# Linformer attention and a gated feed-forward layer in one kernel: single load buffers, q of batch 1 transposed by DMA, denominators once per head, projections moved, 64x32 tiles

## The chip, the core and the metric

The kernel runs on one core of one Trainium2 chip. The metric is the device time of one execution in microseconds. Before the change the median of eight runs is 517.92 us (517.8 to 520.12).

## What is computed

Eight batches of eight heads, 1024 positions, head size 64. k and v are projected along the sequence to 64 rows, q attends to these 64 rows, and the result, with the heads side by side (8192 tokens of 512 numbers), goes through a feed-forward layer of 2048 with a quick-gelu.

```python
k_proj = np.einsum('ks,bhsd->bhkd', E, k)
v_proj = np.einsum('ks,bhsd->bhkd', F, v)
scores = scale * np.matmul(q, k_proj.transpose(0, 1, 3, 2))
scores = scores - np.max(scores, axis=-1, keepdims=True)
attn = np.exp(scores)
attn = attn / (np.sum(attn, axis=-1, keepdims=True) + 1e-09)
attn_out = np.matmul(attn, v_proj)
...
x = attn_out.transpose(0, 2, 1, 3).reshape(B * S, H * D)
h = x @ w_in
out = (h * (1.0 / (1.0 + np.exp(-1.702 * h)))) @ w_out
```

The kernel leaves out the maximum and the small addend in the denominator; inputs and outputs are float32, the matmuls work on bfloat16.

## The kernel before

The 8192 tokens are worked in 16 blocks of 512, two to a batch. Block j runs the feed-forward layer for its tokens: `ffn1` (L295), sixteen groups of four full matmuls whose results ACT turns into gelu, then `ffn2` (L313), eight half groups of eight full matmuls, two for each of four output tiles. The matmuls of a block are 128, each 128x128 by 512 columns. The attention of later blocks is placed between these groups by hand: `at(j, slot, f)` (L344) files a function under block j and a slot, and the main loop (L419) calls what is filed after each group. Slots 0 to 15 follow the groups of ffn1, `O` = 16 is the slot after the first half group of ffn2, `O + 7` the last. Every engine works through its own instructions in this program order; nothing reorders them.

For one block h of 512 tokens the attention is:

- `proj(b)` (L139), once per batch: k and v times E and F, 16 matmuls of 128x64 tiles in pairs. `kv_out(b)` (L184) casts the results on DVE, and for b above 1 SP issues a DMA transpose of k into `kts`. For batch 1, `k_tr` (L161) does it on PE.
- q: for batches 0 and 1 `q_tr` (L195) transposes on PE through PSUM with a DVE copy (L211), in four steps per batch; from batch 2 on `q_dma` (L214) is one DMA transpose on the SP queue.
- `scores(h, u)` (L227), u = 0, 1: `four` (L221), that is four matmuls on 64x64 tiles, then two exponentials on ACT into `expT` (L239).
- `norm(h, u)` (L250), for h from 3: `four` with a matrix of ones for the denominators, which come out repeated over 64 rows each (`d_ps`), `four` with v for the values (`n_ps`), and on DVE a reciprocal of 512 columns (L259) and a product (L260) for each of two tiles, into `xT`.
- For h up to 2, `tok` (L267) and `x_tr` (L282) do the same with tokens on the rows.

A burst is what one slot holds of scores and norm. From block 3 on there are two bursts in each block, in slots O and O + 5, each with scores of block j + 3 and norm of block j + 2.

Loads are issued by POOL in program order (`load`, L65): k and v of a batch by one DMA each, q by eight. `ldpool` has two buffers for each of k, v and q (and one, `q0_sb`, for q of batch 0), and the loads of batch b are called two batches ahead; a load waits until its buffer was read for the last time. The SP queue carries the outputs of each block (L340) and the DMA transposes, in order.

PSUM is eight banks: four for `f_ps` (feed-forward, scores, projections and transposes in turn), two for `d_ps`, two for `n_ps`. A tile that is asked for takes the buffer that was given back first in program order.

Of the kernel before, what the change touches and what calls it, by code (L numbers as in the profile page):

```python
# [9 lines left out]
F32 = mybir.dt.float32  # L10
# [7 lines left out]
def kernel(ctx, tc, q, k, v, E, F,  # L18
# [18 lines left out]
    ldpool = ctx.enter_context(tc.tile_pool(name="ldpool", bufs=2))  # L37
# [4 lines left out]
    ps_n = ctx.enter_context(tc.tile_pool(name="ps_n", bufs=2, space=PSUM))  # L42
    ctx.enter_context(tc.manual_schedule())
# [8 lines left out]
    def load_kv(src, dst, b, name, hs=H, js=0, jn=J):  # L52
        if b not in dst:
            dst[b] = ldpool.tile([P, H, J, D], BF16, name=name, bufs=1 if name == "q0_sb" else 2)
        sv = src[b].rearrange("h (p j) d -> p h j d", p=P)
        for h, n in [(h, hs) for h in range(0, H, hs)] if isinstance(hs, int) else hs:
            nc.gpsimd.dma_start(out=dst[b][:, h:h + n, js:js + jn], in_=sv[:, h:h + n, js:js + jn])  # L57
# [79 lines left out]
    kvps, kbs, qT, expT, xT = {}, {}, {}, {}, {}  # L137
# [57 lines left out]
    def q_tr(b, g):  # L195
        def go():
            if g == 0:
                qT[b] = att.tile([P, J, HP, P], BF16, name="qT")
            t_ps = f_tile([P, 2, HP, P], BF16)
            for jj in range(2):  # L200
                j = 2 * g + jj
                if b == 0:
                    for h in range(H):
                        r = h % 2 * D
                        nc.tensor.transpose(t_ps[r:r + D, jj, h // 2, :], qt[0][:, h, j, :], ident)  # L205
                else:
                    for p in range(HP):
                        nc.tensor.transpose(
                            t_ps[:, jj, p, :],
                            qt[b][:, j, 2 * p:2 * p + 2, :].rearrange("s t d -> s (t d)"), ident)  # L210
            nc.vector.tensor_copy(qT[b][:, 2 * g:2 * g + 2], t_ps)  # L211
        return go

    def q_dma(b):  # L214
        def go():
            qT[b] = att.tile([P, J, HP, P], BF16, name="qT")
            nc.sync.dma_start_transpose(out=qT[b].rearrange("r j p s -> r (j p) s"),
                                        in_=qt[b].rearrange("s j h d -> s (j h d)"))
        return go

    def four(outs, lhsTs, rhss):  # L221

        for i, ro in ((0, (LO, HI)), (1, (HI, LO))):
            for ri, r in zip((LO, HI), ro):
                nc.tensor.matmul(outs[i][r], lhsTs[i][ri], rhss[i][ri], start=True, stop=True)  # L225

    def scores(h, u, half=None):  # L227
        b, c = divmod(h, NB2)
        j0, n = (c * JB, JB) if half is None else (c * JB + half * JB // 2, JB // 2)
        ts = slice(j0 * P - c * TB, (j0 + n) * P - c * TB)  # L230

        def go():
            if h not in expT:
                expT[h] = att.tile([P, HP, TB], BF16, name="expT", bufs=3)
            s_ps = [f_tile([P, n * P]) for _ in range(2)]
            four(s_ps, [kts[b % 2][:, 2 * u + i, :] for i in range(2)],
                 [qT[b][:, j0:j0 + n, 2 * u + i, :] for i in range(2)])
            for i in range(2):
                nc.scalar.activation(expT[h][:, 2 * u + i, ts], s_ps[i], AF.Exp, scale=scale)  # L239
        return go  # L240
# [8 lines left out]

    def norm(h, u):  # L250
        def go():
            e = [expT[h][:, 2 * u + i, :] for i in range(2)]
            d_ps = [ps_d.tile([P, TB], F32, name="d_ps") for _ in range(2)]
            four(d_ps, [ones, ones], e)
            n_ps = [ps_n.tile([P, TB], F32, name="n_ps") for _ in range(2)]
            four(n_ps, [vqs[h // NB2 % 2][:, 2 * u + i, :] for i in range(2)], e)
            for i in range(2):
                rden = att.tile([P, TB], F32, name="rden")
                nc.vector.reciprocal(rden, d_ps[i])  # L259
                nc.vector.tensor_tensor(x_of(h)[:, 2 * u + i, :], n_ps[i], rden, op=ALU.mult)  # L260
# [83 lines left out]
    def at(j, slot, *fs):  # L344
        fill.setdefault((j, slot), []).extend(fs)
# [9 lines left out]
    for u in range(2):  # L355
        scores(0, u, 0)()
    v_out(0, proj0(1, 4, 2), 2, 1)
    for p in range(3):
        tok(0, p, 0)()
    v_out(0, proj0(1, 6, 2), 3, 1, nc.scalar.copy)  # L360
    for p in range(3):
        x_tr(0, p, 0)()
    tok(0, 3, 0)()
    q_tr(0, 1)()
# [17 lines left out]
    at(1, 4, proj(1))  # L382
    at(1, 5, kv_out(1))
    at(1, 7, lambda: k_tr(1, kbs[1], 0), q_dma(2))
    for g in range(4):
        at(1, 8 + 2 * g, q_tr(1, g))
# [8 lines left out]
    at(2, 1, norm(3, 0))  # L395
    at(2, 11, norm(3, 1))
    for b in range(2, B):
        j = max(2, NB2 * b - 3)
        at(j, 2, proj(b))
        at(j, 3, kv_out(b))  # L400
        if b > 2:
            at(NB2 * b - 4, O, q_dma(b))
    for j in (1, 2):
        at(j, O + 5, gelu_table)
    at(2, O + 5, norm(4, 0))
    at(3, 4, norm(4, 1))
    for j in range(3, NBLK - 2):
        for u in range(2):
            if j + 3 < NBLK:
                at(j, O + 5 * u, scores(j + 3, u))  # L410
            at(j, O + 5 * u, norm(j + 2, u))
        if j + 3 < NBLK:
            at(j, O + 6, gelu_table)
# [48 lines left out]
```

The softmax here doesn't subtract the row's maximum and nothing guards it: scores larger than these inputs give would overflow.

## Time and profile before

| what | value |
|---|---|
| median of 8 runs | 517.92 us |
| the profiled execution | 517.8 us |
| its span, first to last instruction | 516.0 us |
| granted TensorE clock, mean | 0.999 |
| first ffn1 matmul (block 0) | 21.03 us |
| blocks 1, 2, 3 begin | 55.4, 90.84, 123.96 us |
| matmuls of ffn1 and ffn2, L301 and L333, busy | 226.6 and 225.1 us |
| DVE reciprocals L259 | 52 of 3353 ns |
| DMA moved | 53.78 MB, 104 GB/s over the span |

The span is what the profile shows from the first instruction to the last; the 1.8 us around it belong to the measured time. A start time in the text is counted from the start of the span. In the profile an engine's busy time is the union of its instructions; PE's matmuls overlap, so what a group of them costs is read from the distance between starts and not from the length of one. "PEld" are the weight loads, which run beside matmuls. Where an instruction waited, the profile names in brackets for how long and for whom. For DMAs, SPq and POOLq rows show when the queue's engine issued them, and "us to landing" how long from there to the completion.

### The profile page before, as it was taken

What the parts mean: (1) busy time and instruction counts of PE and PEld (TensorE: products, weight loads), DVE (VectorE), ACT (ScalarE), POOL (GpSimd) and SP (SyncE); (2) the same over time, 40 slices, a digit from 0 to 9 for tenths busy, and PEclk for the clock granted to TensorE, in tenths of its full rate; (3) what the DMA queues carried; (4) which work ended last, traced back from release to release, by engine and by line L of the source; (5) the groups of instructions that cost most, each with busy time, mean ns of one, the idle gap of its engine ahead of it and who ended that gap; (6) DMA issues with size and microseconds to landing.
All of it is one profiled execution on the core that took longest, in us unless ns stands there. A gap on an engine that the chain in (4) does not pass through costs nothing.

```text
span 516.0 us, 6679 instructions
## 1 busy us (share of the span) xinstructions
PE 504.6 (98%) x2806; PEld 233.4 (45%) x2856; DVE 251.2 (49%) x231; ACT 263.8 (51%) x439; POOL 77.3 (15%) x96
## 2 busy tenths in 40 slices
PE   7899999999999999999999999999999999999997
PEld 3584454434444444444444444444444444444444
DVE  2633324766684672818557282755818275560000
ACT  1575454555646456474555645465473646344351
POOL 7442620831510024000510000000000000000000
PEclk9999999999999999999999999999999999999999
DMA  9999999999996039550694211060200101010102
GB/s 169 197 203 206 219 176 154 196 188 159 239 152 163 1 93 171 108 123 0 152 176 120 50 49 39 0 164 0 85 2 1 81 1 81 1 82 1 81 1 82
DMA packets 113950, 53.78 MB, mean 104 GB/s; under 512 B 87680, under 2 KB 111488, under 8 KB 112000
## 3 DMA queue, kind: packets, MB, share of 16 engines
q0 software_dynamic: 84384, 29.37, 50.4%
q1 hardware_dynamic: 29456, 23.73, 16.7%
q8 instruction: 22, 0.36, 0.3%
q10 hardware_dynamic: 80, 0.26, 0.2%
q14 instruction: 8, 0.07, 0.0%
HBM read 59.24 MB, written 16.78 MB: 147 GB/s over the span
## 4 chain that ended last, share of the span: by engine, by line
PE 85%; DMA 11%; POOL 2%; issue 1%; DVE 0%; DVEq 0%; POOLq 0%
PE f_ps L333 40%; PE f_ps L301 38%; DMA v_sb<-in_v_dram 7%; DMA q_sb<-in_q_dram 5%; PE f_ps L144 2%; PE f_ps L225 2%; PE d_ps L225 1%; PE n_ps L225 1%; POOL q_sb L63 1%; PE f_ps L325 1%; POOL k_sb L57 0%; POOL v_sb L57 0%; PE n_ps L287 0%; PE d_ps L272 0%; POOL q_sb L57 0%
## 5 line engine op out<-in xcount | busy, mean ns | idle before, releaser
L259 DVE RECIPROCAL rden<-d_ps 128x512 f32<-128x512 f32 x52 | 174.4, 3353 | 149.0 <-PE d_ps L225 149.0
L301 PE MATMUL f_ps<-xT,w_in_sb 128*128 128x512 bf16 (+1 forms) x1066 | 226.6, 366 | 1.2
L333 PE MATMUL f_ps<-w_out_sb,gT 128*128 128x512 bf16 x981 | 225.1, 379 | 1.7 <-issue 0.3
L304 ACT ACTIVATE gT<-f_ps 128x512 bf16<-128x512 f32 (+1 forms) x268 | 153.6, 575 | 85.2 <-PE f_ps L301 84.3
L301 PEld LDWEIGHTS <-w_in_sb 128*128 128x128 bf16 x1088 | 104.6, 98 | 115.9 <-issue 4.3
L333 PEld LDWEIGHTS <-gT 128*128 128x128 bf16 x1008 | 95.8, 98 | 120.3 <-issue 11.0
L336 ACT COPY o_sb<-f_ps 128x512 f32<-128x512 f32 x63 | 36.9, 586 | 133.5 <-PE f_ps L333 120.1
L63 POOL DMA_DIRECT2D q_sb<-in_q_dram x56 | 49.1, 907 | 67.4 <-DMA k_sb<-in_k_dram 27.4
L239 ACT ACTIVATE expT<-f_ps 128x512 bf16<-128x512 f32 (+1 forms) x68 | 35.2, 575 | 14.1 <-PE f_ps L225 14.1
L260 DVE TENSOR_TENSOR xT<-n_ps,rden 128x512 bf16<-128x512 f32 x52 | 36.0, 692 | 5.4
L327 DVE COPY o_sb<-f_ps 128x256 f32<-128x256 f32 x1 | 0.4, 425 | 50.9 <-PE f_ps L325 50.9
L57 POOL DMA_DIRECT2D k_sb<-in_k_dram x9 | 7.9, 874 | 102.9 <-PE f_ps L144 101.2
L239 ACT ACT_TABLE_LOAD x13 | 16.7, 1283 | 4.7 <-PE f_ps L225 4.5
L243 ACT ACT_TABLE_LOAD x14 | 18.0, 1283 | 0.2
L225 PE MATMUL f_ps<-qT,kt 64*64 64x512 bf16 (+1 forms) x136 | 13.8, 386 | 0.4 <-ACT expT L239 0.4
L144 PE MATMUL f_ps<-v_sb,eft 128*64 128x512 bf16 x56 | 13.4, 382 | 0.0
L144 PE MATMUL f_ps<-k_sb,eft 128*64 128x512 bf16 x56 | 13.4, 382 | 0.0
L211 DVE COPY qT<-f_ps 128x1024 bf16<-128x1024 bf16 x8 | 5.5, 692 | 12.4 <-PE f_ps L205 6.8
L277 DVE RECIPROCAL rd<-d_ps 128x4 f32<-128x4 f32 x22 | 3.8, 175 | 15.5 <-PE d_ps L272 15.4
L225 PEld LDWEIGHTS <-kt 64*64 64x64 bf16 x136 | 4.0, 103 | 14.3 <-issue 13.8
L225 PE MATMUL d_ps<-expT,ones 64*64 64x512 bf16 x104 | 10.2, 381 | 0.0
L225 PE MATMUL n_ps<-expT,vq 64*64 64x512 bf16 x104 | 10.0, 376 | 0.0
(57 smaller groups left out, 128.1 us busy)
## 6 DMA issues: line engine op xcount, KB each, us to landing
out_dram<-o_sb SPq DMA_DIRECT2D x15, 1024.0 KB, 4.2
k_sb<-in_k_dram POOLq DMA_DIRECT2D x7, 1024.0 KB, 13.8
v_sb<-in_v_dram POOLq DMA_DIRECT2D x7, 1024.0 KB, 10.8
q_sb<-in_q_dram POOLq DMA_DIRECT2D x56, 128.0 KB, 11.1
w_in_sb<-in_moe_w_in_dram POOLq DMA_DIRECT2D x8, 256.0 KB, 12.4
w_out_sb<-in_moe_w_out_dram POOLq DMA_DIRECT2D x4, 512.0 KB, 15.0
k_sb<-in_k_dram POOLq DMA_DIRECT2D x2, 512.0 KB, 7.5
out_dram<-o_sb SPq DMA_DIRECT2D x3, 256.0 KB, 2.0
```

The costliest lines, as they stand in the source:

```text
L57: nc.gpsimd.dma_start(out=dst[b][:, h:h + n, js:js + jn], in_=sv[:, h:h + n, js:js + jn])
L63: nc.gpsimd.dma_start(out=qt[b][:, j], in_=qv[:, j])
L144: nc.tensor.matmul(kvps[b][r], eft[:, j, e * KP:(e + 1) * KP], (kt, vt)[e][b][:, :, j, :], start=(j == 0), stop=(j == J - 1))
L225: nc.tensor.matmul(outs[i][r], lhsTs[i][ri], rhss[i][ri], start=True, stop=True)
L239: nc.scalar.activation(expT[h][:, 2 * u + i, ts], s_ps[i], AF.Exp, scale=scale)
L243: nc.scalar.preload_act_table(AF.Gelu_apprx_sigmoid)
L259: nc.vector.reciprocal(rden, d_ps[i])
L260: nc.vector.tensor_tensor(x_of(h)[:, 2 * u + i, :], n_ps[i], rden, op=ALU.mult)
L301: nc.tensor.matmul(h_ps, w_in_sb[:, kc, fc * P:(fc + 1) * P], xT[j][:, kc, ts], start=(kc == 0), stop=(kc == KC - 1))
L304: nc.scalar.activation(gts[j][:, fc, ts], h_ps, AF.Gelu_apprx_sigmoid)
L333: nc.tensor.matmul(o_ps[n], gts[j][:, fc, n * P:(n + 1) * P], w_out_sb[:, fc, :], start=(fc == 0), stop=(fc == FC - 1))
L336: nc.scalar.copy(osb[j][:, n, :], o_ps.pop(n))
```

## The change

It has six parts.

- k, v and q have one load buffer each. A batch's loads therefore wait until the batch before was projected (k, v) and transposed (q).
- q of batch 1 is transposed by two DMAs on SP, each for half of the tokens, filed in slot (1, 1); the branch of `q_tr` for later batches goes, and `q_dma(2)` moves from (1, 7) to (1, O + 7).
- `four` becomes `eight`: the same products with tiles of 64 rows and 32 columns, two for each 64x64 tile.
- From h = 4 on `norm` is split. `sums(h)` gets the denominators of all eight heads with one set of eight 64x32 tiles, takes two reciprocals on DVE, writes four rows of them to DRAM (`rdr`) and reads them back repeated over 64 rows (`rbc`), both by DMAs on SP. `values(h, u)` multiplies with v and then, on DVE, with `rbc`. sums(h) is filed in (h - 2, O), values(h, 0) in (h - 2, O + 6), values(h, 1) in (h - 1, O).
- `proj(1)` moves to (1, 10), `proj(3)` to (3, 6) beside values(4, 0), and proj(4) to proj(7) from (2b - 3, 2) to (2b - 4, O + 6), ahead of that slot's burst. The second burst moves from O + 5 to O + 6. `q_dma(b)` of batches 4 to 7 moves from (2b - 4, O) to (2b - 4, 2).
- At the start, tok and x_tr of block 0's first half are ordered differently among the projections of v.

```diff
-    ldpool = ctx.enter_context(tc.tile_pool(name="ldpool", bufs=2))
+    ldpool = ctx.enter_context(tc.tile_pool(name="ldpool", bufs=1))
+    dram = ctx.enter_context(tc.tile_pool(name="dram", bufs=2, space=bass.MemoryType.DRAM))
...
-            dst[b] = ldpool.tile([P, H, J, D], BF16, name=name, bufs=1 if name == "q0_sb" else 2)
+            dst[b] = ldpool.tile([P, H, J, D], BF16, name=name)
...
-                j = 2 * g + jj
-                if b == 0:
-                    for h in range(H):
-                        r = h % 2 * D
-                        nc.tensor.transpose(t_ps[r:r + D, jj, h // 2, :], qt[0][:, h, j, :], ident)
-                else:
-                    for p in range(HP):
-                        nc.tensor.transpose(
-                            t_ps[:, jj, p, :],
-                            qt[b][:, j, 2 * p:2 * p + 2, :].rearrange("s t d -> s (t d)"), ident)
+                for h in range(H):
+                    r = h % 2 * D
+                    nc.tensor.transpose(t_ps[r:r + D, jj, h // 2, :], qt[0][:, h, 2 * g + jj, :], ident)
             nc.vector.tensor_copy(qT[b][:, 2 * g:2 * g + 2], t_ps)
         return go
 
-    def q_dma(b):
-        def go():
-            qT[b] = att.tile([P, J, HP, P], BF16, name="qT")
-            nc.sync.dma_start_transpose(out=qT[b].rearrange("r j p s -> r (j p) s"),
-                                        in_=qt[b].rearrange("s j h d -> s (j h d)"))
-        return go
-
-    def four(outs, lhsTs, rhss):
+    def q_dma(b, j0=0, n=J):
+        def go():
+            if j0 == 0:
+                qT[b] = att.tile([P, J, HP, P], BF16, name="qT")
+            nc.sync.dma_start_transpose(out=qT[b][:, j0:j0 + n].rearrange("r j p s -> r (j p) s"),
+                                        in_=qt[b][:, j0:j0 + n].rearrange("s j h d -> s (j h d)"))
+        return go
+
+    def eight(outs, lhsTs, rhss):
         for i, ro in ((0, (LO, HI)), (1, (HI, LO))):
-            for ri, r in zip((LO, HI), ro):
-                nc.tensor.matmul(outs[i][r], lhsTs[i][ri], rhss[i][ri], start=True, stop=True)
+            for c in range(0, KP, 32):
+                for ri, r in zip((LO, HI), ro):
+                    nc.tensor.matmul(outs[i][r.start + c:r.start + c + 32], lhsTs[i][ri, c:c + 32], rhss[i][ri],
+                                     start=True, stop=True)
 
...
+    def sums(h):
+
+
+        def go():
+            d_ps = [ps_d.tile([P, TB], F32, name="d_ps") for _ in range(2)]
+            for p in range(HP):
+                for e in range(2):
+                    r = HI if (p + e) % 2 else LO
+                    nc.tensor.matmul(d_ps[e][32 * p:32 * p + 32], ones[r, :32], expT[h][r, p, :], start=True, stop=True)
+            rden = att.tile([P, 2, TB], F32, name="rden")
+            for e in range(2):
+                nc.vector.reciprocal(rden[:, e, :], d_ps[e])
+            rdr = dram.tile([HP, 2, TB], F32, name="rdr")
+            nc.sync.dma_start(out=rdr, in_=rden[0:P:32])
+            rbc[h] = att.tile([P, HP, TB], F32, name="rbc")
+            for e, r in enumerate((LO, HI)):
+                nc.sync.dma_start(out=rbc[h][r], in_=rdr[None, :, e, :].to_broadcast([D, HP, TB]))
+        return go
+
     def norm(h, u):
         def go():
             e = [expT[h][:, 2 * u + i, :] for i in range(2)]
             d_ps = [ps_d.tile([P, TB], F32, name="d_ps") for _ in range(2)]
-            four(d_ps, [ones, ones], e)
+            eight(d_ps, [ones, ones], e)
             n_ps = [ps_n.tile([P, TB], F32, name="n_ps") for _ in range(2)]
-            four(n_ps, [vqs[h // NB2 % 2][:, 2 * u + i, :] for i in range(2)], e)
+            eight(n_ps, [vqs[h // NB2 % 2][:, 2 * u + i, :] for i in range(2)], e)
             for i in range(2):
-                rden = att.tile([P, TB], F32, name="rden")
-                nc.vector.reciprocal(rden, d_ps[i])
-                nc.vector.tensor_tensor(x_of(h)[:, 2 * u + i, :], n_ps[i], rden, op=ALU.mult)
+                rd = att.tile([P, TB], F32, name="rdn")
+                nc.vector.reciprocal(rd, d_ps[i])
+                nc.vector.tensor_tensor(x_of(h)[:, 2 * u + i, :], n_ps[i], rd, op=ALU.mult)
+        return go
+
+    def values(h, u):
+        def go():
+            n_ps = [ps_n.tile([P, TB], F32, name="n_ps") for _ in range(2)]
+            eight(n_ps, [vqs[h // NB2 % 2][:, 2 * u + i, :] for i in range(2)],
+                  [expT[h][:, 2 * u + i, :] for i in range(2)])
+            for i in range(2):
+                nc.vector.tensor_tensor(x_of(h)[:, 2 * u + i, :], n_ps[i], rbc[h][:, 2 * u + i, :], op=ALU.mult)
         return go
...
     for u in range(2):
         scores(0, u, 0)()
+    for p in range(2):
+        tok(0, p, 0)()
     v_out(0, proj0(1, 4, 2), 2, 1)
-    for p in range(3):
-        tok(0, p, 0)()
+    x_tr(0, 0, 0)()
     v_out(0, proj0(1, 6, 2), 3, 1, nc.scalar.copy)
-    for p in range(3):
-        x_tr(0, p, 0)()
+    tok(0, 2, 0)()
+    x_tr(0, 1, 0)()
     tok(0, 3, 0)()
+    x_tr(0, 2, 0)()
     q_tr(0, 1)()
     x_tr(0, 3, 0)()
...
-    at(1, 4, proj(1))
-    at(1, 5, kv_out(1))
-    at(1, 7, lambda: k_tr(1, kbs[1], 0), q_dma(2))
-    for g in range(4):
-        at(1, 8 + 2 * g, q_tr(1, g))
+    at(1, 10, proj(1))
+    at(1, 11, kv_out(1))
+    at(1, 13, lambda: k_tr(1, kbs[1], 0))
+    at(1, 1, q_dma(1, 0, JB), q_dma(1, JB, JB))
...
-    at(2, 1, norm(3, 0))
-    at(2, 11, norm(3, 1))
-    for b in range(2, B):
-        j = max(2, NB2 * b - 3)
-        at(j, 2, proj(b))
-        at(j, 3, kv_out(b))
-        if b > 2:
-            at(NB2 * b - 4, O, q_dma(b))
     for j in (1, 2):
         at(j, O + 5, gelu_table)
-    at(2, O + 5, norm(4, 0))
-    at(3, 4, norm(4, 1))
-    for j in range(3, NBLK - 2):
+    at(1, O + 7, q_dma(2))
+    at(2, 1, norm(3, 0))
+    at(2, 2, proj(2), kv_out(2))
+    at(2, 11, norm(3, 1))
+    at(2, O + 5, sums(4))
+    at(2, O, q_dma(3))
+    at(3, 6, proj(3), kv_out(3), values(4, 0))
+    for b in range(4, B):
+        j = NB2 * b - 4
+        at(j, O + 6, proj(b), kv_out(b))
+        at(j, 2, q_dma(b))
+    for j in range(3, NBLK - 1):
         for u in range(2):
             if j + 3 < NBLK:
-                at(j, O + 5 * u, scores(j + 3, u))
-            at(j, O + 5 * u, norm(j + 2, u))
+                at(j, O + 6 * u, scores(j + 3, u))
+        at(j, O, values(j + 1, 1))
+        if j + 2 < NBLK:
+            at(j, O, sums(j + 2))
+            at(j, O + 6, values(j + 2, 0))
         if j + 3 < NBLK:
-            at(j, O + 6, gelu_table)
+            at(j, O + 7, gelu_table)
```

## The prediction, made before the changed kernel had run

> **What bounds the kernel now.** I read the page from its first part down: busy time by engine, then the chain that ended last.
>
> ```profile
> span 516.0 us, 6679 instructions
> ...
> PE 504.6 (98%) x2806; PEld 233.4 (45%) x2856; DVE 251.2 (49%) x231; ACT 263.8 (51%) x439; POOL 77.3 (15%) x96
> ...
> PE 85%; DMA 11%; POOL 2%; issue 1%; DVE 0%; DVEq 0%; POOLq 0%
> ```
>
> PE is busy for 98% of the span, carries the chain from 72 us to the end, and DVE and ACT stand at half. So a microsecond taken from PE is a microsecond of the span, unless PE then waits; one taken from DVE is worth nothing by itself. The DMA share of the chain lies before 72 us, where PE is busy too: the chain view follows loads there, but the stage windows below leave PE idle for only 0.2 to 0.4 us per block after the first 21 us.
>
> Next, busy time in windows cut at the starts of the blocks: a block with two bursts of attention work, one that also holds a projection, and one with the feed-forward layer alone. The columns are window, length, then busy time of PE, PEld, DVE, ACT, POOL, clock, DMA share, GB/s.
>
> ```profile
> 155.96:185.34 29.38, 29.22 (x151) 12.85 (x152) 16.01 (x9) 16.43 (x26) 0.00 (x0) 1.00 0.29 72
> 185.34:216.68 31.34, 31.18 (x167) 13.60 (x168) 17.55 (x12) 16.54 (x26) 8.75 (x10) 1.00 1.06 137
> 457.20:484.80 27.60, 27.50 (x127) 12.51 (x128) 4.34 (x3) 11.89 (x20) 0.00 (x0) 1.00 0.10 39
> ```
>
> The last gives the price of a full-size matmul: 27.60/128 = 0.2156 us. The first costs 1.78 us more, for two bursts of three groups each (scores, sums, values). How long one group takes is seen in PE's timeline of one burst:
>
> ```profile
> 262.31 1.24 PE L333 MATMUL f_ps<-w_out_sb,gT 128*128 128x512 bf16 x5
> 263.49 0.41 PE L225 MATMUL f_ps<-qT,kt 64*64 64x512 bf16 x4
> 263.73 0.39 PE L225 MATMUL d_ps<-expT,ones 64*64 64x512 bf16 x4
> 263.94 0.39 PE L225 MATMUL n_ps<-expT,vq 64*64 64x512 bf16 x4
> 264.26 0.60 PE L333 MATMUL f_ps<-w_out_sb,gT 128*128 128x512 bf16 x2
> ```
>
> Groups of four 64x64 tiles start 0.21 to 0.24 us apart: the four run at once, for the price of one matmul. Six groups are 6 x 0.2156 = 1.29 us, so each burst pays (1.78 - 1.29)/2 = 0.24 us to enter and leave the 64x64 layout. A projection adds 31.34 - 29.38 = 1.96 us: 8 pairs x 0.2156 = 1.73, and again 0.23 us for its own layout.
>
> **What the Trainium skill says.** TensorEngine Tiling (Array Packing), Tiling Modes: 64x32 gives eight independent tiles, and changing the tiling mode drains TensorE. The trace agrees on the drain (0.24 us) and on independence for four tiles; it holds no 32-column tile. TensorE: Matmul & The Clock Gate, Measured speedup vs the span model: a packed set lasts one matmul plus about 4 ns per further tile, up to sixteen tiles. The four tiles above agree; for eight I work out an estimate of 16 ns more per group. DMA: Bandwidth & Descriptors, Queues, rings and completion order: each engine takes turns between queues packet by packet. The packet counts of two DMA windows agree, 117 to 121 us with both queues at work (first two lines), and 161 to 164 us with a transpose alone (last line):
>
> ```profile
> q1 hardware_dynamic: 1661, 0.43, 81.1%
> q0 software_dynamic: 1661, 0.21, 79.6%
> ```
> ```profile
> q1 hardware_dynamic: 2593, 0.66, 114.7%
> ```
>
> So a q transpose (1 MB in 256 B packets, 4096) moves 860 packets per us alone, 415 beside a q load, and 146 beside a k or v load (585 in the window 80 to 84 us).
>
> **The change, part by part.**
>
> 1. *q of batch 1.* Four q_tr(1) leave PE:
>
> ```profile
> 65.45 0.61 PE L208 MATMUL f_ps<-ident,q_sb 128*128 128x128 bf16 x8
> 65.89 1.89 PE L301 MATMUL f_ps<-xT,w_in_sb 128*128 128x512 bf16 x8
> ```
>
> From start to start 0.44 us, so 4 x 0.44 = **-1.76 us**. In their place SP issues two half transposes at slot (1,1). They queue behind block 0's output (issued at 56.2) and q1's load (k2's load follows it into the ring at about 58). With 2048 packets each at 860 per us, and 3 us from issue to first packet (157.3 to 160.2 in the DMA records, with the output ahead), the halves land near 67 and 71 us; scores(2,0) needs the first at about 73 us, scores(3,0) the second near 78. Covered by 6 to 7 us. Even a whole transpose at its slow, contended 15 us would end just in time.
>
> 2. *One buffer.* k2 now waits for proj(1), moved to slot 10: that ends near 66.4 us. q2 waits for both transposes (71), then eight loads at 0.88 us issue and 0.85 us of data (128 KB at 155 GB/s), then v2 (1 MB at 205 GB/s, 5 us): lands near 88 us. proj(2) comes at about 92. 4 us to spare. The same chain later: k3 after proj(2) (94), q3 after q_dma(2), v3 about 118, proj(3) at (3,6) near 128. From batch 4 on the loads have over 30 us for 20 us of work. Freed early, the DMA engines are quiet while q1 is transposed.
>
> 3. *Sums once per head.* Per head from 4 to 15 two d groups (64 columns of ones) become one group of eight 64x32 tiles: 12 groups x 0.2156 = **-2.59 us**. DVE loses 24 reciprocals at 3.35 us, 80 us, worth nothing on this path. The new way back is long: from the start T of ffn2, sums end at T+2.6, two products (0.69 each), two reciprocals (3.35 each), rdr (16 KB; 2.0 us, as the 256 KB outputs), and two rbc of 512 KB (5 us; between 4.2, as a 1 MB output, and 8.4): T+17.7. values(h,0) are on PE at T+13.5, so DVE stands some 4 us at its product. Behind it DVE has nothing before the next block's burst at T+31; proj and kv_out are issued ahead of it in the same slot. n_ps is wanted again at T+31. So it costs nothing; if the DMAs took 14 us longer, PE would begin to feel it. On SP, rdr and rbc wait ahead of the block's output, which is ready at T+14.6: two output buffers cover that.
>
> 4. *Merged bursts.* proj(3) to proj(7) move next to a 64x32 burst: three layout changes for four, each half of 0.24: 5 x 0.12 = **-0.6 us**. norm(4,1) at (3,4) is one burst less, values(15,1) at (14,O) one more: zero. With proj in slot O+6, ffn1 of the next block takes the buffer freed first, kvps: DVE has done with it 1.7 us after proj, PE asks after 2.3 us (scores, values, half an ffn2). No stall. The gelu table load after the last ffn2 copy delays the first gelu to about 2.7 us into the block, and PE asks for that buffer at 3.46 us.
>
> 5. *Eight for four.* 70 full and 4 half groups remain (34 of scores, 4 of norm(3), 12 sums, 24 values; 86 before). The cost per group is not in the trace: below, 0, since one, two (proj) and four tiles all start 0.216 us apart; above, 0.2156, if only four run at once. The skill's 4 ns gives 16 ns. I take 5 ns, as that issue time should mostly hide under the group before: **+0.4 us**.
>
> 6. *Start.* tok of pairs 0 and 1 go ahead of proj0(4,2), so DVE's first reciprocal comes about 0.8 us sooner, but its casts of vx for pair 2 and ACT's for pair 3 follow later in the line; x_tr(0,3) moves from 20.9 to about 20.6, and ffn1's last quarter, which waits for ACT's copy at 21.23, with it: **-0.3 us** (from +0.2 to -0.7).
>
> 7. *SP's order in block 2.* Before, the transpose of q2 ran at 75; now it goes out after block 1's output (89.4), ahead of kt(2).
>
> ```profile
> 101.78 1.19 SPq L190 DMA_TRANSPOSE kt<-k_b  x1
> ...
> 109.59 0.11 PEld L225 LDWEIGHTS <-kt 64*64 64x64 bf16 x4 [0.42 <-DMA kt<-k_b]
> ```
>
> kt(2) was just in time before: k_b waits for DVE's norm(3,0), 8.1 us, unchanged. In the new time scores(4,0) come at 107.6. q_dma(2): output packets to 93, 2.6 us alone (2240 packets), 6.7 us beside k3's load (980), 1.0 us alone: ends about 103, SP free at 102.3; kt(2) then takes 2.7 us to its first packet (as at 190.6) and about 1.5 more: 106.5. Expected wait 0; if contention lasts, up to 3.5 us. I take **+0.2**.
>
> **Sum.** -1.76 - 2.59 - 0.6 - 0.3 + 0.4 + 0.2 = -4.65 us. The profiled run took 517.8 us (span 516.0, 1.8 around it): 513.2. The median of the eight runs is 517.92, so this is 4.7 us, 0.9%, below it. I count 0.2%, about 1 us, as what can be told from no change.
>
> **Rivals.**
>
> *A new wait gives part back (14%).* The wait of part 7 at scores(4,0) at its 3.5 us, or a late v2: 513.2 + 3.3 = 516.5. For it: kt(2) was already last before. Against: k_b's own delay is the same, and loads are quieter.
>
> *Eight tiles don't run at once (17%, the slower side).* If the array takes only four at a time, 70 x 0.2156 + 4 x 0.108 = 15.5 us: 513.2 - 0.4 + 15.5 = 528.3. It decides from (4.65 + 0.4)/74 = 68 ns per group on. For it: no 32-column tile in the trace, and every right-hand side is streamed twice. Against: four streams run free of charge, and 16 weight loads and matmuls of narrow transposes at line 205 went through in 0.57 us (32.83 to 33.40).
>
> *The change doesn't do what it says (7%).* The transposes of q1 land late, or the merged bursts stall on PSUM, and PE waits for what it saved: 517.5, 4% within 0.2%, 3% slower. Against: 6 us of cover.
>
> **How the numbers follow.** The forecast has 62%, with its own range 511.8 to 514.6 (start and tile issue at their ends). With the first rival faster has 0.76, same 0.04, slower 0.20 (17 and 3). To leave out no more than 2 in 10 the range goes from 511.8 to 518.0.
>
> **What would show it.** Right: windows of later blocks at 29.1 and 31.0 us; sums at one group of eight per head, starts 0.22 us apart; no L208; 24 reciprocals fewer; DVE waiting for rbc, PE not. Wrong: groups of eight spaced 0.28 us or more; PE idle before scores(4,0) or scores(2,0) on a transpose; PE idle before ffn1 on kvps or an f_ps buffer at a block's start.

## The result, and the profile after

The changed kernel takes 513.79 us (median of 11 runs, 512.66 to 515.21) where the kernel before, measured beside it, takes 517.99 us (32 runs). The ratio of runs is 0.9908 with an interval of 0.9896 to 0.992: 4.2 us, 0.9%, faster. The forecast was 513.2 us, with a range of 511.8 to 518.0.

The page of the changed kernel, its span, the busy time by engine and the shares of the chain that ended last:

```profile
span 513.0 us, 7127 instructions
...
PE 498.2 (97%) x3022; PEld 231.2 (45%) x3072; DVE 165.0 (32%) x203; ACT 262.5 (51%) x439; POOL 77.3 (15%) x96
...
PE 94%; DMA 3%; issue 1%; DVE 1%; ACT 1%; ACTq 0%
```

DVE lost 86 us of work and ACT about 1, and the time fell by about 4: the kernel is still bound by PE, now with 94% of the chain. The windows of a block with a projection, the next block and block 14 (columns as before: window, length, PE, PEld, DVE, ACT, POOL, clock, DMA share, GB/s) show where it fell:

```profile
155.31:186.32 31.01, 30.64 (x182) 13.59 (x184) 10.59 (x9) 16.29 (x26) 1.93 (x3) 1.00 0.61 133
186.32:215.49 29.17, 28.80 (x167) 12.77 (x169) 9.06 (x6) 16.39 (x26) 6.82 (x8) 1.00 1.27 171
453.92:481.99 28.07, 27.96 (x136) 12.57 (x137) 2.58 (x4) 11.89 (x20) 0.00 (x0) 1.00 0.21 61
```

The projection now lies in the even block, so it is the pair that compares: 31.34 + 29.38 = 60.72 us before, 31.01 + 29.17 = 60.18 now, 0.54 less. Block 14 is longer, 28.07 for 27.60, since one values group moved into it.

Cut at the first matmul of every ffn1 and ffn2 in PE's timeline, the whole difference is this (us):

| stretch | before | after | difference |
|---|---|---|---|
| first matmul of v's projection to the first ffn1 | 6.18 | 6.03 | -0.15 |
| block 1, ffn1 (q of batch 1, proj(1)) | 17.88 | 16.09 | -1.79 |
| block 1, ffn2 (scores, tok and x_tr; no sums, no values) | 17.40 | 17.40 | 0.00 |
| block 2, ffn2 | 16.03 | 15.81 | -0.22 |
| block 3, ffn1 | 16.43 | 16.11 | -0.32 |
| block 3, ffn2 | 15.57 | 15.97 | +0.40 |
| blocks 4 to 11, four pairs | 60.72 | 60.18 | -0.54 each, -2.16 |
| blocks 12 and 13, ffn2, each | 15.57, 15.14 | 15.35, 14.92 | -0.22 each, -0.44 |
| block 14, ffn2 | 13.81 | 14.26 | +0.45 |
| first ffn1 matmul to last matmul | 491.16 | 487.06 | -4.10 |
| last matmul to the end of the span | 3.84 | 3.49 | -0.35 |

Stretches that are not in the table differ by 0.02 us at most. The sum from v's projection on is -0.15 - 4.10 - 0.35 = -4.60 us. The profiled run itself came out only 3.0 us shorter in span (513.0, a time of 514.8), because its v projection began 1.6 us later (16.45 us for 14.85): the granted clock over the first 10 us was 0.88, before 1.00, and the page's PEclk row starts with 8, before with 9.

What one burst costs now, in PE's timeline (start, length, line, operation, and the count of instructions):

```profile
409.83 1.89 PE L359 MATMUL f_ps<-w_out_sb,gT 128*128 128x512 bf16 x8
411.65 0.41 PE L222 MATMUL f_ps<-qT,kt 64*32 64x512 bf16 x8
411.88 0.40 PE L222 MATMUL n_ps<-expT,vq 64*32 64x512 bf16 x8
412.09 0.40 PE L256 MATMUL d_ps<-expT,ones 64*32 64x512 bf16 x8
```

Groups of eight 64x32 tiles start 0.21 to 0.23 us apart, where the groups of four 64x64 started 0.21 to 0.24 us apart.

The one new wait is in block 3. First PE's weight loads, then SP's issues before it, in the timeline of the changed kernel (for SP the length is how long the queue's engine was at the instruction):

```profile
141.78 0.11 PEld L222 LDWEIGHTS <-kt 64*32 64x32 bf16 x8 [1.04 <-DMA kt<-k_b]
```

```profile
116.13 10.19 SPq L212 DMA_TRANSPOSE qT<-q_sb  x1
126.51 0.63 SPq L261 DMA_DIRECT2D rdr<-rden  x1
128.60 1.32 SPq L264 DMA_DIRECT2D rbc<-rdr  x2
129.97 0.59 SPq L366 DMA_DIRECT2D out_dram<-o_sb  x1
132.07 3.38 SPq L191 DMA_TRANSPOSE kt<-k_b  x1
```

scores(6, 0) waited for the k of batch 3. Ahead of its transpose in the same queue stand q's transpose, the reciprocals out and back (1 MB) and block 2's output (1 MB). These are the reciprocals of sums(4), which the change files in slot O + 5 of block 2; only from h = 5 on is it slot O. The idle 1.04 us are 0.62 us more than the same place shows where kt is early: there 0.42 us of PEld idle stay, which belong to the change of layout.

### The profile page after: what moved, and what is told of

Same layout as the page of the kernel before. It is cut to its first block, busy times and chain, and to the rows that moved or that the text cites. A ratio compares the mean times of both kernels' runs of the same rounds, so it can differ in the third digit from the quotient of the medians.

```text
span 513.0 us, 7127 instructions
## 1 busy us (share of the span) xinstructions
PE 498.2 (97%) x3022; PEld 231.2 (45%) x3072; DVE 165.0 (32%) x203; ACT 262.5 (51%) x439; POOL 77.3 (15%) x96
## 4 chain that ended last, share of the span: by engine, by line
PE 94%; DMA 3%; issue 1%; DVE 1%; ACT 1%; ACTq 0%
PE f_ps L359 42%; PE f_ps L327 42%; PE f_ps L145 3%; PE f_ps L222 2%; DMA kt<-k_b 2%; PE n_ps L222 1%; DMA ef_f<-in_E_dram 1%; PE f_ps L124 1%; PE n_ps L313 1%; PE f_ps L153 1%; PE d_ps L298 1%; PE d_ps L256 1%; PE f_ps L204 0%; PE f_ps L351 0%; DVE x_sb L305 0%
## 5 line engine op out<-in xcount | busy, mean ns | idle before, releaser
L359 PE MATMUL f_ps<-w_out_sb,gT 128*128 128x512 bf16 x976 | 221.0, 379 | 4.1 <-issue 3.6
L330 ACT ACTIVATE gT<-f_ps 128x512 bf16<-128x512 f32 (+1 forms) x268 | 151.2, 575 | 64.6 <-PE f_ps L327 63.6
L286 DVE TENSOR_TENSOR xT<-n_ps,rbc 128x512 bf16<-128x512 f32 x48 | 30.9, 686 | 210.7 <-PE n_ps L222 124.9
L259 DVE RECIPROCAL rden<-d_ps 128x512 f32<-128x512 f32 x24 | 78.7, 3322 | 7.8 <-PE d_ps L256 7.8
L189 DVE CAST k_b<-f_ps 64x512 bf16<-64x512 f32 x7 | 4.8, 681 | 36.7 <-PE f_ps L145 36.7
L276 DVE RECIPROCAL rdn<-d_ps 128x512 f32<-128x512 f32 x4 | 13.4, 3353 | 5.0 <-PE d_ps L222 5.0
L222 PE MATMUL f_ps<-qT,kt 64*32 64x512 bf16 (+1 forms) x272 | 13.8, 374 | 0.9 <-DMA kt<-k_b 0.5
L222 PEld LDWEIGHTS <-kt 64*32 64x32 bf16 x272 | 3.9, 88 | 14.9 <-issue 13.8
L222 PE MATMUL n_ps<-expT,vq 64*32 64x512 bf16 x208 | 10.4, 378 | 0.0
L305 DVE TENSOR_TENSOR x_sb<-d_ps,rd 128x256 bf16<-128x256 f32 x22 | 9.3, 425 | 0.8
```

Source lines behind the costliest of these rows:

```text
L222: nc.tensor.matmul(outs[i][r.start + c:r.start + c + 32], lhsTs[i][ri, c:c + 32], rhss[i][ri], start=True, stop=True)
L259: nc.vector.reciprocal(rden[:, e, :], d_ps[e])
L276: nc.vector.reciprocal(rd, d_ps[i])
L330: nc.scalar.activation(gts[j][:, fc, ts], h_ps, AF.Gelu_apprx_sigmoid)
L359: nc.tensor.matmul(o_ps[n], gts[j][:, fc, n * P:(n + 1) * P], w_out_sb[:, fc, :], start=(fc == 0), stop=(fc == FC - 1))
```

## The experiments

Three of the twelve kernels (the two combinations at the end and the changed kernel again) were timed in five rounds; of the others there is one trace and one time. A stretch of PE's timeline that an edit leaves alone repeats to 0.05 us from run to run, except in block 3's ffn2, in the start, in block 0's ffn1 (17.57 to 17.98 us) and after the last matmul, so one trace settles differences of 0.1 us there. Where the texts say "per head" or "head 3", h is meant: a block of 512 tokens with all of its eight heads.

### Four 64x64 tiles again, sums kept

```diff
-            eight(d_ps, [ones, ones], e)
+            four(d_ps, [ones, ones], e)
```

and so for every other call of `eight`, in scores, norm and values; `four` is defined again as before the change.

> The changed kernel with scores, norm and values on four 64x64 tiles again; only sums keeps 64x32. Theory (PE work alone sets the time, and a group of eight tiles costs the same 0.216 us as one of four): a block without sums keeps its length, ffn2 of block 1 stays 17.40 us; in blocks 4 to 13 the burst with sums pays one more layout change, 0.12 us, so a pair of blocks grows from 60.18 us to about 60.4. Rival (eight tiles do cost something, hidden in the sum): bursts of scores become shorter by 5 to 16 ns per group, ffn2 of block 1 falls to 17.34 to 17.38 us and the pair of blocks is unchanged or shorter.

Measured: block 1's ffn2, four groups of scores and no sums, is 17.40 us with four tiles and with eight. So the eight are free. The pair of blocks grew from 60.18 to 60.43 us, since sums still has 64x32 tiles and a burst now changes layout in its middle. PE's timeline of this kernel:

```profile
169.86 0.41 PE L219 MATMUL f_ps<-qT,kt 64*64 64x512 bf16 x4
170.10 0.39 PE L219 MATMUL n_ps<-expT,vq 64*64 64x512 bf16 x4
170.42 0.41 PE L261 MATMUL d_ps<-expT,ones 64*32 64x512 bf16 x8
```

From scores to values 0.24 us, from values to sums 0.32: one change between 64x64 and 64x32 costs about 0.12 us. The ffn2 of eleven of the twelve blocks with sums grew by it, 0.12 to 0.13 us each; block 3's grew by 0.36, with a longer wait for kt. The theory came true.

### q of batch 1 on PE again

```diff
...
-    at(1, 1, q_dma(1, 0, JB), q_dma(1, JB, JB))
+    for g in range(4):
+        at(1, 6 + 2 * g, q_tr(1, g))
```

The lines left out give `q_tr` its branch for later batches back.

> The changed kernel with q of batch 1 transposed on PE again (four groups of eight transposes in slots 6, 8, 10, 12 of block 1), all else the same. Theory: ffn1 of block 1 grows from 16.09 to 17.85 us (4 x 0.44) and nothing else moves, since the DMA transposes were hidden. Rival (what the two DMAs bring is partly lost in later waits on loads, or gained by an earlier load of batch 2): the rest of the kernel moves by more than 0.3 us, above all block 2 and ffn2 of block 3.

Measured: block 1's ffn1 went back from 16.09 to 17.88 us, +1.79, and from block 0's ffn2 to the last matmul no other stretch moved by more than 0.1 (the start did, by 0.3 us, as it does from run to run). Part 1 of the prediction is worth just what it takes off PE.

### Sums and values together again, twice per block

```diff
-    at(2, O + 5, sums(4))
...
-    at(3, 6, proj(3), kv_out(3), values(4, 0))
+    at(3, 6, proj(3), kv_out(3), norm(4, 0))
...
-        at(j, O, values(j + 1, 1))
-            at(j, O, sums(j + 2))
-            at(j, O + 6, values(j + 2, 0))
+        at(j, O, norm(j + 1, 1))
+            at(j, O + 6, norm(j + 2, 0))
```

> The changed kernel with denominators and values together again from head group 4 on (norm in the slots of values, eight tiles kept, no DMA of reciprocals). Theory: 12 more groups of 0.216 us, 2.6 us more in blocks 2 to 14 (a block pair 60.18 to 60.61 us), DVE busy 80 us more at no further cost, and the wait of scores(6,0) in ffn2 of block 3 (0.6 us) goes, because the reciprocals' DMAs no longer stand ahead of the transpose of k on SP: net about +2.0 us. Rival (relief of DVE is what pays): a block pair grows by clearly more than 0.43 us, over 0.6.

Measured: 517.08 us; the twelve groups came back at 0.21 to 0.22 us each. DVE had its 80 us of reciprocals again and PE never waited for them: the windows from block 4 on grew by the groups and nothing else. Block 3's wait was gone (ffn2 15.57 us): here no rdr and rbc stand ahead of kt, which SP issued in 1.18 us at 131.89, and which landed 7.3 us later:

```profile
kt<-k_b SPq DMA_TRANSPOSE x1, 7.3
```

### The projection of batch 3 earlier, and later

```diff
-    at(3, 6, proj(3), kv_out(3), values(4, 0))
+    at(3, 4, proj(3), kv_out(3), values(4, 0))
```

A later kernel has slot 10 in the same line.

> The changed kernel with the projection of batch 3 and values(4,0) in slot 4 of block 3 in place of slot 6. Theory: the wait of 0.6 us at scores(6,0) comes from the transpose of k for batch 3 being issued 9 us before it is needed behind 2 MB in its own queue; issued 1.7 us earlier it lands in time, ffn2 of block 3 falls from 15.97 to 15.35 us. Rival (it is the output of block 2 and the reciprocals' DMAs in front that set the landing, and they do not move): ffn2 of block 3 stays above 15.7 us.

> The projection of batch 3 is issued at slot 10 of block 3 instead of slot 6, four ffn1 groups of 0.86 us, 3.45 us, later. Theory: kt of batch 3 had 0 us of slack, so nearly the whole shift becomes a wait of the first scores of block 3's ffn2: 15.35 to 15.97 us grows to 18.4 to 19.4 us, and the time by 2.9 to 3.5 us. Rival, as the prediction had it (3 us of slack ahead of kt, and a wait in the first trace that came from something else): 15.4 to 16.3 us as before, and the time within 0.7 us.

Measured: block 3's ffn2 took 15.42 us with slot 4, but the same stretch varies among kernels that leave block 3 alone: 15.97, 15.88, 15.48 and 15.35 us in four of them at slot 6. One trace at slot 4 therefore showed nothing by itself. Two later kernels with slot 4 had 15.35 both times; with slot 10 it was 16.84. Both expectations for slot 10 missed: not 3 us more, and not nothing, but 1.5 us over a kernel without the wait. The timeline of the late kernel, SP and then PE's weight loads, says why:

```profile
128.71 0.59 SPq L366 DMA_DIRECT2D out_dram<-o_sb  x1
134.33 1.21 SPq L191 DMA_TRANSPOSE kt<-k_b  x1
...
141.46 0.11 PEld L222 LDWEIGHTS <-kt 64*32 64x32 bf16 x8 [1.92 <-DMA kt<-k_b]
```

Issued some 3.4 us later, the transpose held SP for 1.21 us instead of 2.75 (a run of the changed kernel whose kt was issued at 130.91) and landed 7.1 us after its issue, against 9.7 us in the first trace. That is about what it took with no reciprocals ahead of it (7.3 us, above). So about 2 us of the shift were time that the early transpose had spent behind the DMAs ahead of it, and 1.5 us came out as a wait. The Trainium skill (DMA: Bandwidth & Descriptors, Queues, rings and completion order) has descriptors of one queue consumed in order on each DMA engine; the trace agrees, as far as these lengths tell it. So the slack of kt(3) at slot 6 is nil to half a microsecond, and the wait is 0 to 0.9 us by run (the longest in the kernel with four tiles); what sets it from run to run is open.

The order on SP isn't all of it. A kt with no load beside it lands in 2.3 us. In all these runs the load of batch 4's k, which waits for proj(3), is issued 0.2 to 0.4 us before kt; before the change it was 0.5 us, and kt(3) took 6.6 us. It had more time then: proj(3) stood in slot 2, 3.4 us earlier.

### The reciprocals spread three times

```diff
-            for e, r in enumerate((LO, HI)):
+            for e, r in ((0, LO), (1, HI)) * 3:
                 nc.sync.dma_start(out=rbc[h][r], in_=rdr[None, :, e, :].to_broadcast([D, HP, TB]))
```

The same bytes are written three times, each time after the one before.

> The changed kernel with each repeated read of the reciprocals done three times over (24 MB more of DMA writes, same data). Theory: DVE waits some 10 us longer at the products, PE does not wait for it from block 4 on: block pairs stay at 60.18 us within 0.05. Only ffn2 of block 3 grows, by 4 us or more, since these DMAs stand ahead of the transpose of k for batch 3 on SP. Rival (the way of the reciprocals through DRAM is close to the limit): every block from 4 on grows.

Measured: 562.12 us, and the expectation was wrong. Not only block 3 grew (ffn2 by 18.0 us) but the ffn2 of blocks 5, 7 and 9 too, by 8.4 to 9.9, and that of blocks 6, 12, 13 and 14 by 0.3 to 0.8. The waits, SP's and PE's timeline around the start of block 5's ffn2, and PE's of block 12:

```profile
DVE xT L286 <- DMA rbc<-rdr: 247.7, 12, 22.8
...
PEld L222 <- DMA kt<-k_b: 38.6, 4, 17.5
```

```profile
197.27 0.55 SPq L261 DMA_DIRECT2D rdr<-rden  x1
199.13 17.65 SPq L264 DMA_DIRECT2D rbc<-rdr  x6
216.88 1.23 SPq L191 DMA_TRANSPOSE kt<-k_b  x1
...
226.55 0.63 PE L222 MATMUL f_ps<-qT,kt 64*32 64x512 bf16 x8 [6.66 <-DMA kt<-k_b]
...
457.61 0.40 PE L222 MATMUL n_ps<-expT,vq 64*32 64x512 bf16 x4 [0.20 <-DVE xT L286]
```

DVE waits for rbc 247.7 us in all (76.1 in the changed kernel). What PE feels of it first is kt, which goes out on SP only when the six DMAs of rbc are issued. In blocks 6, 12, 13 and 14 no kt is late, and there PE meets the other limit, n_ps banks that DVE's products still hold: in block 12 they began 20.3 us after rdr was issued, where the changed kernel has 9.5. So the nearer limit of a slow rbc is SP's order, and DVE's products come next.

The waits of PE at kt, 17.0, 6.7, 6.9 and 6.0 us, are not the whole of the growth: over these four stretches the granted clock was 0.75 to 0.86, and the matmuls after each wait ran slower for some microseconds.

### The projections alone, the start alone

```diff
-        at(j, O + 6, proj(b), kv_out(b))
+        at(j + 1, 2, proj(b))
+        at(j + 1, 3, kv_out(b))
```

> The changed kernel with the projections of batches 4 to 7 back in slot 2 of the block after, away from the bursts. Theory: each pays one layout change more, 0.11 us: a block pair grows from 60.18 to 60.29 us, the kernel by 0.44 us. Rival (moving them next to a burst brought nothing or cost a stall on a PSUM buffer): pairs stay or become shorter.

Measured: 513.79 us; ffn2 of the even block lost 1.85 us and ffn1 of the odd one gained 1.95, 0.10 to 0.11 us per pair. One change of layout less for each of four projections: 0.42 us.

```diff
-    for p in range(2):
-        tok(0, p, 0)()
     v_out(0, proj0(1, 4, 2), 2, 1)
-    x_tr(0, 0, 0)()
+    for p in range(3):
+        tok(0, p, 0)()
     v_out(0, proj0(1, 6, 2), 3, 1, nc.scalar.copy)
-    tok(0, 2, 0)()
-    x_tr(0, 1, 0)()
+    for p in range(3):
+        x_tr(0, p, 0)()
     tok(0, 3, 0)()
-    x_tr(0, 2, 0)()
     q_tr(0, 1)()
```

> The changed kernel with the first half of block 0 in the order of the kernel before. Theory: from the projection of the first four heads of v to the first ffn1 matmul it takes 6.18 us, as before, in place of 6.03: 0.15 us. Rival (the new order brings the 0.3 us or more that I forecast, and the slower clock of that profiled start hid it): 6.3 us or more at full clock.

Measured: 514.91 us, and 6.18 us from v's projection to the first ffn1 matmul. The old order gave 6.18 in all three kernels that had it. The new order gave 6.02 to 6.04 in five traces and 6.35 to 6.62 in six, with no difference among them in these instructions; the changed kernel itself had 6.03 once and 6.62 once. So the 0.15 us of the first trace is no gain to count on; the mean of the eleven is 6.26.

### Single buffers in the kernel before

```diff
-    ldpool = ctx.enter_context(tc.tile_pool(name="ldpool", bufs=2))
+    ldpool = ctx.enter_context(tc.tile_pool(name="ldpool", bufs=1))
...
-            dst[b] = ldpool.tile([P, H, J, D], BF16, name=name, bufs=1 if name == "q0_sb" else 2)
+            dst[b] = ldpool.tile([P, H, J, D], BF16, name=name)
```

> The kernel before with one buffer each for loaded k, q and v, and nothing else changed. Theory: single buffers bring no time and cost little, as loads still land before they are used: within 0.3 us from the first ffn1 matmul to the last matmul (491.16 us before). Rival (single buffers are part of the gain, because batch 2 no longer loads while q of batch 1 is needed): shorter by over 0.3 us. Second rival: the transpose of q of batch 2, now later and beside the load of v, holds up the transpose of k and scores(4,0): block 2 grows by 1 us or more.

Measured: 521.26 us, with 494.27 us from the first ffn1 matmul to the last matmul, 3.1 over the kernel before, so the theory missed. 1.02 us is block 2's ffn2, where scores(4, 0) wait for a kt that comes late. The place and the size are those of the second rival and of part 7 of the prediction, the cause is not: q's transpose had left SP at 94.7 us, kt went out at 104.17, and beside the loads of batch 3 it took 8.8 us to land, where it took 7.5 in the kernel before. The other 2.09 us are in block 1's ffn1. PE's timeline of the kernel before, and then of this one:

```profile
69.80 0.61 PE L208 MATMUL f_ps<-ident,q_sb 128*128 128x128 bf16 x8
70.24 1.67 PE L301 MATMUL f_ps<-xT,w_in_sb 128*128 128x512 bf16 x7
71.97 0.61 PE L208 MATMUL f_ps<-ident,q_sb 128*128 128x128 bf16 x8
```

```profile
70.10 0.61 PE L208 MATMUL f_ps<-ident,q_sb 128*128 128x128 bf16 x8
70.95 1.02 PE L301 MATMUL f_ps<-xT,w_in_sb 128*128 128x512 bf16 x4 [0.24 <-ACT gT L304]
72.65 1.02 PE L301 MATMUL f_ps<-xT,w_in_sb 128*128 128x512 bf16 x4 [0.69 <-ACT gT L304]
74.36 0.61 PE L208 MATMUL f_ps<-ident,q_sb 128*128 128x128 bf16 x8 [0.69 <-ACT gT L304]
```

These are not waits for a load. PE, ACT and DVE have the same instructions in the same order in both programs, but three ffn1 and q_tr groups wait for the gelu that has only just been issued: the program gave their tiles other f_ps banks, the same one to three groups in a row (four of PE's waits name ACT where they named DVE, or the other way round). Why another number of load buffers moves the choice of a PSUM bank is open. In the changed kernel, where q_tr(1) and its tiles are gone, neither wait is there.

### What is left on the table

The ledger named three small things, so a kernel took all of them, and a second took those that had looked safest after the first had missed. The changed kernel itself ran beside the first.

```diff
...
-    at(2, 1, norm(3, 0))
-    at(2, 2, proj(2), kv_out(2))
-    at(2, 11, norm(3, 1))
+    at(2, 2, proj(2), kv_out(2), sums(3))
+    at(2, O, values(3, 0))
+    at(2, O + 3, values(3, 1))
...
-    at(3, 6, proj(3), kv_out(3), values(4, 0))
+    at(3, 4, proj(3), kv_out(3), values(4, 0))
...
-    for j in range(3, NBLK - 1):
+    for j in range(3, NBLK - 2):
...
+    at(NBLK - 3, O + 6, values(NBLK - 1, 1, ps_d, "d_ps"))
```

> The changed kernel with what the ledger says it still gives away: head 3 is normalised with one shared sums product instead of twice (three groups of eight rather than four, 0.216 us each, and one visit of the PE to the 64x32 layout fewer at 0.24 us), the second values group of block 15 moves into the burst at (13, O + 6) with two idle banks of another pool (one visit of the layout fewer, 0.24 us), and the projection of batch 3 is issued at slot 4 of block 3 rather than at slot 6, so that its kt lands 1.7 us earlier (the wait of 0 to 0.9 us in block 3 goes). My theory, a sum of group times, layout visits and that one wait: 0.45 us less in block 2, 0.24 us less in block 14, 0 to 0.9 us less in block 3; from the first ffn1 matmul to the last matmul 485.5 to 486.5 us (487.06 in the changed kernel), and a time 0.7 to 1.5 us under the changed kernel of the same call. Rival: a layout visit costs nothing by itself and the 0.24 us belonged to the waits around it; then only about 0.2 us is gained in block 2 and nothing in block 14. Second rival: the values of head 3, now behind the DMA that spreads the reciprocals, come late for block 3's ffn1, and block 2 ends 1 us or more later.

> The changed kernel itself once more, for the comparison with the version before on the same chip, and for another sample of its one new wait. Theory: 0.992 of the time before within 0.001; block 3's ffn2 between 15.35 and 16.3 us (the kt of batch 3 lands within a microsecond of the moment it is wanted, on either side), all other blocks within 0.05 us of the first trace. Rival: the wait is a fixed property of the order of issue, and block 3 shows 15.97 us again.

Measured: the first is slower, 520.9 us, 1.005 of before (1.0034 to 1.0065). The gains came: 0.98 us in block 2's ffn1, of which 0.43 moved to its ffn2 with the two values groups, and 0.24 in blocks 13 and 14 together. But block 2's ffn2 grew by 8.4 us: the second rival, which had named 1 us or more. SP's and PE's timeline of it:

```profile
102.08 0.62 SPq L261 DMA_DIRECT2D rdr<-rden  x1
107.58 1.31 SPq L264 DMA_DIRECT2D rbc<-rdr  x2
```

```profile
107.35 0.40 PE L222 MATMUL n_ps<-expT,vq 64*32 64x512 bf16 x8
...
119.61 1.21 PE L222 MATMUL n_ps<-expT,vq 64*32 64x512 bf16 x8 [5.79 <-DVE xT L286]
```

Beside the loads of batch 3, rdr took 5.5 us and rbc 11 more; DVE's product waited for it until 118.86, the n_ps banks with it, and PE with them. This wait and the moved groups are 6.2 of the 8.4 us; the granted clock over the stretch was 0.86, and the matmuls after the wait ran slower. The changed kernel beside it took 513.68 us, 0.9922 of before (0.9896 to 0.9947); its block 3 had 15.35 us, so the wait is not fixed, and from block 1 on no other stretch moved.

```diff
...
-    at(2, 1, norm(3, 0))
-    at(2, 2, proj(2), kv_out(2))
+    at(2, 2, proj(2), kv_out(2), norm(3, 0))
...
+    at(NBLK - 3, O + 6, values(NBLK - 1, 1, ps_d, "d_ps"))
```

with proj(3) at slot 4 and the loop one block shorter, as above.

> The changed kernel with the three small moves that cost no new wait: the first norm of head 3 goes into the visit of the 64-row layout that the projection of batch 2 makes one group later (0.12 to 0.24 us less in block 2), the second values group of block 15 goes into the burst at (13, O + 6) in two idle banks (0.24 us less over blocks 13 and 14), and the projection of batch 3 is issued at slot 4 of block 3 (the wait of 0 to 0.9 us for its kt goes, as in the run that moved it alone). Theory: from the first ffn1 matmul to the last matmul 485.8 to 486.3 us, and a median 0.4 to 1.1 us under the changed kernel's. Rival: head 3's norms, two visits of the array with 6.5 us of reciprocals behind each, still tie PE to VectorE as the shared sums of head 3 did, and block 2 grows instead by some microseconds.

Measured: 514.9 us, 0.994 of before (0.9927 to 0.9954), not better than the changed kernel. Again blocks 13 and 14 gave 0.24 us and block 3 had no wait, but block 2's ffn1 grew by 1.25 us. PE's timeline at norm(3, 1):

```profile
102.15 0.40 PE L222 MATMUL d_ps<-expT,ones 64*32 64x512 bf16 x4
102.94 0.40 PE L222 MATMUL d_ps<-expT,ones 64*32 64x512 bf16 x4 [0.40 <-DVE rdn L276]
102.96 0.40 PE L222 MATMUL n_ps<-expT,vq 64*32 64x512 bf16 x4
103.74 0.40 PE L222 MATMUL n_ps<-expT,vq 64*32 64x512 bf16 x4 [0.38 <-DVE xT L277]
```

norm(3, 0)'s reciprocals, 3.35 us each, now began behind the casts of k and v, at 95.47 us, 6.3 us into the block; in the changed kernel it is 92.60, 2.3 us into it. norm(3, 1), nine ffn1 groups later, met its d_ps and n_ps banks still in use. The rival had the mechanism right, at a smaller size than it named. No kernel here beat the changed one; moving the values group into the earlier burst is worth 0.24 us in both kernels, but was not run without the rest.

## Why the prediction was right, step by step

The sum was -4.65 us and the ledger gives -4.60. Two large terms, parts 1 and 3, were right to 0.03 us each. The small ones missed in both directions, by 0.1 to 0.4 us each, and that these misses cancel is luck.

- *Part 1, q of batch 1 (-1.76).* Measured -1.79, and +1.79 when undone alone. The transposes were in time: no wait at scores(2, 0) or scores(3, 0).
- *Part 2, one buffer (0).* Right in the changed kernel, where PE never waits for a load. It isn't free by itself: in the kernel before, single buffers cost 3.1 us, of which 1.0 is a late kt and 2.1 the bank choice. The other parts are what pays for it.
- *Part 3, sums (-2.59).* Measured as twelve groups of 0.216 us. DVE's 80 us were worth nothing from block 4 on, as said. rbc arrived 19.6 us after the start of ffn2 (the first product at 188.75 us, ffn2 at 169.12), not 17.7; PE did not feel it. The limit that the prediction gave, DMAs some 14 us longer, is there: with rbc tripled, PE waited a little for n_ps in blocks 12 to 14, where rbc came 11 us later. But it looked at n_ps and DVE only, and the tripled rbc showed SP's order, with kt behind rbc, to be the nearer limit in the blocks that have a kt.
- *Part 4, merged bursts (-0.6).* The mechanism was right, with 0.12 us for a change of layout; the count was not. Four projections gave 0.43 us (0.42 when undone alone). At block 3 the vanished burst of norm(4, 1) and the merged projection are one saved change, 0.11 us, where the prediction counted a merge of 0.12 and a burst of 0.24, set against the 0.24 us that values(15, 1) costs in block 14. In all -0.3.
- *Part 5, eight for four (+0.4).* It is 0.00 us per group: block 1's ffn2 is 17.40 us with four and with eight. The rival that the array takes four at a time is out. The 4 ns per further tile that the Trainium skill states (TensorE: Matmul & The Clock Gate, Measured speedup vs the span model) are there inside a group: the eight tiles at 411.65 start 3 to 4 ns apart, 24 ns from the first to the last. They don't add to the distance between groups of 512 columns, so the prediction's 16 ns per group, and the 5 ns that it took, were too much.
- *Part 6, start (-0.3).* -0.15 in the first trace, +0.08 in the mean of eleven: no gain is shown.
- *Part 7, SP's order (+0.2).* The wait came, but not at kt(2): scores(4, 0) showed no wait on it, and q's transpose held SP only to 98.9 us, not to 102.3. It came one batch later, at kt(3), 0.62 us in the first trace and 0 to 0.9 by run, so that the size was met by luck. This is the step that failed: the prediction followed the queue in block 2 and gave the loads of batch 3 to proj(3), but did not walk the queue from sums(4) to kt(3), where rdr, rbc and block 2's output now stand ahead and proj(3) comes four slots later.
- *Not in the sum.* The end, from the last matmul on, is 0.35 us shorter. Nine of the twelve traces of kernels built on the changed one have 3.49 or 3.50 us there, the other three 3.60 to 3.81; the cause was not tried.

The forecast lies 0.6 us under the median. The start makes that: of the eleven runs seven had a mean clock of 0.999 or 1.0 and took 512.66 to 513.91 us, around the 513.2 of the sum; the four with 0.996 or 0.997 took 514.06 to 515.21. Three traces with 0.997 (the changed kernel's first, the one with norm twice per block, and the one with the old start) have 3.4 us at half clock from 7.7 to 9.2 us on and their first ffn1 matmul at 22.5 to 23.2 us; those with 0.999 or 1.0 have it at 20.8 to 21.6.

## What to carry to other kernels

Where PE is 97% busy, count groups of matmuls and changes of tile layout, and multiply by their starts in the timeline: that gave the two large terms, 4.4 of 4.6 us, to 0.05 us. For every transfer that the change adds, walk the issuing queue to the next transfer that PE waits for, in every stage and not only where the profile before shows a tight one. And before merging bursts, look which engine works through what the burst leaves behind: 0.12 us of layout was paid for tenfold when 3.35 us reciprocals slid behind a projection and its casts.

## What the runs showed that was not expected

- Groups of eight 64x32 tiles, with twice the instructions and every right-hand side read by twice as many tiles, follow each other at the same 0.216 us as groups of four 64x64 tiles and as full matmuls.
- A 64 KB transpose on SP held the queue's engine 1.2 us with nothing just ahead of it and up to 3.4 us behind 2 MB of other transfers; q's 1 MB transposes held it 7 to 10 us.
- Where PE stood for 5.8 to 17.0 us at one place, the granted clock was half for 3.0 to 5.6 us after it went on, and the wait cost 1.5 to 3.0 us more than its own length; after waits of 0.5 to 1.0 us the clock was still 1.00.
- Two reads of 512 KB that spread rows over partitions landed 7.5 us after their issue in a quiet stage (181.26 to 188.75 with the product's start) and 11 us beside the loads of a batch.
- The start is not steady from run to run: the first ffn1 matmul came at 20.8 to 23.2 us in kernels with the same work before it, according to the clock granted in the first 13 us. The Trainium skill (TensorE: Matmul & The Clock Gate, What's actually happening) has the clock at half or full rate, decided over windows of about 3.4 us that don't start with the kernel. The traces agree: four of the fourteen have one stretch of 3.41 us at half clock, beginning at 7.7 to 9.2 us, and the others none in the start. 2.4 us is more than half of what this change brings.
